# Where VectorE sums k, who makes a quarter of the local probabilities' copies, and how the tail of k is copied: attention and mixture of experts on one core

## The chip, the core and the metric

The kernel runs on one core of a Trainium2 chip. The core has five engines, each with its own in-order queue: TensorE (PE: matrix products and transposes, with its weight loads, PEld, beside them), VectorE (DVE), ScalarE (ACT), GpSimd (POOL) and SyncE (SP, which issues most transfers). [...] The metric is the time of one execution on the device in microseconds, the median of several runs.

## The reference

Two stages. Attention for 8 batch elements, 8 heads, 576 positions of 64 numbers: a local part, in which a position sees only its neighbours less than 4 away, and a coarse part over sums of 4 positions, whose output is repeated four times. Then a mixture of 8 experts: each of the 4,608 rows goes to the expert with the largest gate.

```python
q_d, k_d, v_d = (x.reshape(B, H, Sd, 4, D).mean(axis=3) for x in (q, k, v))
out_up = np.repeat(sm_attn(q_d, k_d, v_d), 4, axis=2)
mask = np.abs(pos[:, None] - pos[None, :]) < 4
scores = np.where(mask, scale * np.matmul(q, k.transpose(0, 1, 3, 2)), -1e9)
attn = softmax(scores)                    # max, exp, sum + 1e-09
x = rows(out_up + np.matmul(attn, v))
e_idx = argmax(x @ w_gate + modality_bias[modality_id])
out[e_idx == e] = gate * (np.maximum(x[e_idx == e] @ w1[e], 0) @ w2[e])
```

## The kernel before

**Steps.** Attention goes in 32 steps, n = 4b + hp, four for each batch element b. The work of one step is spread over almost four step times: while step n's q and k are transposed, step n − 1 has its scores, n − 2 its normalization and n − 3 its output. In the notes below the name in brackets is that of the method (and of the tile in the profile).

- PE transposes q and k into PSUM (tp, L275), four blocks each. ScalarE copies them to SBUF, q scaled (qT, L295) and k in two copies of 64x512, one for each half of the partitions (kT, L307). VectorE sums each four neighbouring columns of the same PSUM tile of k (kd, L321; in the call list kd0). The 64 columns that are left over at the end of each step are transposed for two steps together (tpt, L288); ScalarE copies k's part in four copies of 64x64 (L304 and L305), VectorE sums it (kd1, L317).
- The coarse scores (scd, L376) need kd and POOL's sums of q (qe L327, qd L331). VectorE takes their maximum (dm, L381), ScalarE the exponential with its sums (de, L389), POOL the division (nd, L407, which writes de), PE transposes (pdt, L428), ScalarE copies to SBUF (PdT, L436), and PE multiplies with v's sums (vp L263, copied by VectorE to vd at L268; avd L443).
- The local scores (mask and sc, L341 and L349) are 32 wide windows. VectorE takes maximum and difference (lm L356, le L362), ScalarE the exponential (L367), VectorE the sums and their reciprocal (z L393, zr L398 and L399), POOL the product with it (nl, L403, which writes le), VectorE transposes blocks of 32x32 (lt, L414). Then ScalarE makes four copies of 32 partitions each (Pw, L419, j from 0 to 3) into a tile that is zero elsewhere, and PE multiplies with v (avl, L458). VectorE adds coarse and local part (X, L469, a piece of it named late).
- In every fourth step the router runs for a finished batch element: logits (lg L505), copied by ScalarE (LT, L512) and transposed (lgt, L518); VectorE's chain of small operations (L524 to L563, from L to w and so on), PE's ranks (pr, L570 to L574), slots (sl and si, up to L586), and POOL's scatters of row numbers (tab, L615), four or five for a batch element; VectorE transposes rows (R, L600), SP stores them.

**Order.** The order of each engine's queue is not left to a scheduler. `PHASE` gives each method of a step a due time in units of steps; `call(n + p, ...)` collects all calls, and the list is sorted by time and issued in that order, so an engine's queue holds its instructions in the order of their due times. For VectorE the fractions of one step run: zr 0.29, R 0.30, kd0 0.30, lm1 0.34, le1 0.37, L and ch1 0.44 to 0.49, lt 0.508, dm 0.509, kd1 0.54, ch2 0.56, vc 0.66, X 0.66 and 0.69, lm0 0.73, le0 0.84, z 0.90. For POOL: nl 0.45, nd 0.60, qe and qd 0.62, between them scatters at 0.00, 0.20, 0.59 and 0.62 of certain steps.

**Buffers.** PSUM tiles of tag T (three buffers) serve the transposes: tp, tpt, vp, pdt, lgt. A buffer comes free when its last reader is done; for k's transposes that is ScalarE's copies and VectorE's sums. Reads of one PSUM tile by two engines are kept apart by the framework: kd begins when kT's second copy is done.

**After attention**, from about 260 us on, the expert units run: PE does three passes for each product (high and low parts of both factors).

Of the kernel before, what the change touches and what calls it, by code (L numbers as in the profile page):

```python
# [7 lines left out]
F32 = mybir.dt.float32  # L8
# [14 lines left out]
SUB, WIN, KEYS = 24, 32, 30  # L23
BLK = 4 * SUB
NB = 6
PAD = 3
KT = S - SUB + WIN
# [17 lines left out]
NPW = 3  # L45
# [8 lines left out]

PHASE = {
# [22 lines left out]
class Consts:  # L78
    def __init__(s, tc, pool, psum):
        nc = tc.nc  # L80

        s.ps = psum
        pool.tile([128, 48], F32, name="pad")
        s.dummy = pool.tile([128, 128], BF16, name="dummy")
        nc.vector.memset(s.dummy, 0.0)
        s.busy(nc, 12)
        s.ident = pool.tile([128, 128], F32, name="ident")
        make_identity(nc, s.ident)
        s.identb = pool.tile([128, 128], BF16, name="identb")
        make_identity(nc, s.identb)  # L90

        x = pool.tile([128, 1], F32, name="warm")
        nc.vector.memset(x, 0.0)
        nc.scalar.activation(x, x, AF.Exp)
        m = pool.tile([128, WIN], BF16, name="band")
        nc.gpsimd.memset(m, 0.0)
        for j in range(4):
            t = m[32 * j : 32 * j + 32]
            nc.gpsimd.affine_select(out=t, in_=t, pattern=[[1, WIN]], compare_op=ALU.is_ge, fill=NEG, base=0,
                                    channel_multiplier=-1)  # L100
            nc.gpsimd.affine_select(out=t, in_=t, pattern=[[-1, WIN]], compare_op=ALU.is_ge, fill=NEG, base=6,
                                    channel_multiplier=1)
        s.mask = pool.tile([128, NB, WIN], BF16, name="mask")
        nc.vector.tensor_copy(s.mask, m.unsqueeze(1).broadcast_to([128, NB, WIN]))
        nc.vector.memset(s.mask[0:32, 0:2, 0:PAD], NEG)
        s.band = m

        s.pool = pool.tile([128, 32], F32, name="pool")
# [84 lines left out]
class Attention:  # L193


    def __init__(s, tc, ctx, ectx, C, psum, q, k, v):
        s.tc, s.C, s.ps = tc, C, psum
        nc = s.nc = tc.nc
        s.q, s.k, s.v = q, k, v

        s.ld = ectx.enter_context(tc.tile_pool(name="ald", bufs=2, side="right", reuse_waits="tile"))
        s.wk = ctx.enter_context(tc.tile_pool(name="awk", bufs=2, reuse_waits="tile"))
        s.one = ctx.enter_context(tc.tile_pool(name="aone", bufs=1, reuse_waits="tile"))
        s.QK, s.t = {}, {}
        s.vw = [(s.ld, s.one)[j].tile([128, H * NB, D], F32, name=f"vw{j}", bufs=1) for j in range(2)]

        s.qT2 = s.ld.tile([128, 2, S], F32, name="qT", bufs=1)
        s.kB = s.ld.tile([128, 2, 2, KT], F32, name="kT", bufs=1)
        nc.vector.memset(s.kB, 0.0)
        s.mask = s.one.tile([128, NB, WIN], BF16, name="mask")  # L210
        nc.vector.tensor_copy(s.mask, C.band.unsqueeze(1).broadcast_to([128, NB, WIN]))
        nc.vector.memset(s.mask[96:128, NB - 2 :, SUB + PAD : WIN], NEG)
        s.Pw = [s.one.tile([128, 2 * NB, 4, SUB], F32, name=f"Pw{j}") for j in range(NPW)]

        s.De = [s.one.tile([128, 3, 32 * NB], F32, name=f"de{j}") for j in range(3)]
        for j in range(2):
            (nc.vector, nc.gpsimd)[j].memset(s.vw[j], 0.0)

        for j in range(3):
            nc.vector.memset(s.De[j], 0.0)  # L220
# [76 lines left out]
    def kT_(s, n, i):  # L297
        g = n % 2
        p = s.t["tp", "t"][:, 1] if i else s.t["tp", "k", n]
        for a in range(2):  # L300
            r = slice(64 * a, 64 * a + 64)
            if i:
                t = s.kB[r].rearrange("m g a t -> m g (a t)")[:, :, KT * a + PAD : KT * a + PAD + 512 + 64]
                s.nc.scalar.copy(t[:, 0, 512:], p[r, :64])  # L304
                s.nc.scalar.copy(t[:, 1, :64], p[r, 64:])  # L305
            else:
                s.nc.scalar.copy(s.kB[r, g, a, PAD + 64 * g : PAD + 64 * g + 512], p[r])  # L307

# [107 lines left out]
    def Pw_(s, n, j):  # L416

        r = slice(32 * j, 32 * j + 32)
        s.nc.scalar.copy(s.Pw[n % NPW][r, :, j, :SUB], s.t["lt", n][r, :, :SUB])  # L419

    def pdt(s, n, i):

# [850 lines left out]
```

## Time and profile before

| | us |
|---|---|
| median of 3 runs | 694.59 |
| lowest, highest | 693.19, 696.73 |
| the profiled execution | 696.98 |
| its span, first to last instruction | 695.3 |
| PE busy | 649.5 (93%) |
| DVE busy | 403.1 (58%) |
| ACT busy | 379.9 (55%) |
| POOL busy | 238.6 (34%) |

The shares are of the whole span and mix two stages. The attention stage takes the first 260 us, the expert units the rest. Times in the views are microseconds from the span's start. In lists of instructions a line is: start, duration, engine, line of the kernel, operation, out<-in, shape of out<-shape of in, count, and in brackets the idle time of that engine before it with what ended it. Matmuls are pipelined, so a busy PE isn't at its peak.

### The profile page before, as it was taken

The page shows a single profiled execution, that of the slowest core. Times are in us where ns is not written, and L with a number is a line of the kernel's source. Part 1 is how long each engine was busy: PE and PEld are TensorE (multiplying, and loading weights), DVE is VectorE, ACT ScalarE, POOL GpSimd, SP SyncE. Part 2 cuts the span into 40 slices and gives each one's busy share as a digit, 9 for nine tenths or more (in the row PEclk, how much of TensorE's full clock was granted, in tenths as well). Part 3 has the DMA queues.
Part 4 walks back from the last instruction along what each step waited for, and adds up shares of the span by engine and source line. Part 5 has one row for each costly group of instructions (what it writes and reads, how often), then busy time and mean ns, then how long its engine had stood idle before and what let it go on. Part 6 is the DMA issues. An engine that isn't in the chain of part 4 may idle for free. (4 is left out here: it accounts for less than half of the span.)

```text
span 695.3 us, 16717 instructions
## 1 busy us (share of the span) xinstructions
PE 649.5 (93%) x6123; PEld 518.3 (75%) x6123; DVE 403.1 (58%) x938; ACT 379.9 (55%) x884; POOL 238.6 (34%) x302
## 2 busy tenths in 40 slices
PE   7898999888988889998999999999999999999896
PEld 4576666666656667886888888888888888889794
DVE  6688898888879886746444234323452343416610
ACT  4798998887888754452444334433443243425710
POOL 6644563635476564360220300403204012210111
PEclk9899999999999999999999999999999999999999
DMA  9899889998887938397561544616524345155700
GB/s 186 171 179 195 161 182 194 157 206 146 159 172 166 200 81 219 99 309 221 153 210 45 169 152 121 192 51 185 179 81 122 131 137 181 53 136 171 221 29 31
DMA packets 176423, 106.99 MB, mean 154 GB/s; under 512 B 136300, under 2 KB 154770, under 8 KB 176338
## 3 DMA queue, kind: packets, MB, share of 16 engines
q1 hardware_dynamic: 169138, 86.71, 53.9%
q0 software_dynamic: 7200, 19.18, 8.6%
q8 instruction: 50, 0.82, 0.5%
q14 instruction: 35, 0.29, 0.2%
HBM read 86.61 MB, written 19.51 MB: 153 GB/s over the span
## 5 line engine op out<-in xcount | busy, mean ns | idle before, releaser
L833 DVE TENSOR_TENSOR wlo<-raw,whi 128x1024 fp32r<-128x1024 f32 x73 | 87.9, 1227 | 79.6 <-ACT whi L827 72.4
L977 POOL DMA_INDIRECT out_dram<-o,tg x34 | 37.1, 1091 | 250.2 <-ACT o L969 194.6
L923 DVE SCALAR_TENSOR_TENSOR hl<-l,hh 128x512 fp32r<-128x512 f32 x72 | 49.5, 688 | 105.4 <-ACT hh L922 101.7
L922 ACT ACTIVATE hh<-l 128x512 fp32r<-128x512 f32 x72 | 42.6, 596 | 109.8 <-PE l L918 108.2
L966 PE MATMUL l<-whi,hh 128*128 128x512 f32 x256 | 100.2, 395 | 1.9 <-ACT hh L947 1.9
L966 PE MATMUL l<-whi,hl 128*128 128x512 f32 x256 | 99.9, 391 | 0.0
L966 PE MATMUL l<-wlo,hh 128*128 128x512 f32 x256 | 99.8, 391 | 0.0
L918 PE MATMUL l<-xh,whi 128*128 128x512 f32 (+1 forms) x256 | 95.1, 375 | 2.1 <-DVE hl L923 2.1
L918 PE MATMUL l<-xl,whi 128*128 128x512 f32 (+1 forms) x256 | 94.7, 370 | 0.0
L918 PE MATMUL l<-xh,wlo 128*128 128x512 f32 (+1 forms) x256 | 94.6, 370 | 0.0
L827 ACT CAST whi<-raw 128x1024 fp32r<-128x1024 f32 x70 | 71.5, 1051 | 29.6 <-DMA raw<-in_moe_w_dram 16.7
L969 ACT ACTIVATE o<-l,tg 128x512 f32<-128x512 f32 x37 | 25.4, 687 | 97.6 <-PE l L966 69.6
L403 POOL TENSOR_TENSOR le<-le,zr 128x384 f32<-128x384 f32 x32 | 26.6, 831 | 91.3 <-DVE zr L399 84.9
L966 PEld LDWEIGHTS l<-whi,hh 128*128 128x128 f32 x256 | 48.2, 188 | 11.8 <-ACT hh L947 2.2
L918 PEld LDWEIGHTS l<-xh,whi 128*128 128x128 f32 x256 | 48.1, 189 | 11.5 <-DVE hl L923 2.7
L419 ACT COPY Pw<-lt 32x288 f32<-32x288 f32 x128 | 54.5, 426 | 3.4 <-DVE lt L414 1.2
L966 PEld LDWEIGHTS l<-wlo,hh 128*128 128x128 f32 x256 | 48.2, 188 | 10.1
L966 PEld LDWEIGHTS l<-whi,hl 128*128 128x128 f32 x256 | 48.3, 189 | 9.5
L918 PEld LDWEIGHTS l<-xh,wlo 128*128 128x128 f32 x256 | 48.2, 188 | 8.3
L918 PEld LDWEIGHTS l<-xl,whi 128*128 128x128 f32 x256 | 48.3, 189 | 8.0
L896 DVE TENSOR_TENSOR xl<-xt,xh 128x512 fp32r<-128x512 f32 x37 | 24.3, 681 | 38.0 <-ACT xh L894 37.9
L615 POOL DMA_INDIRECT tab<-ig,si x36 | 38.5, 1068 | 20.7 <-DVE si L586 14.5
(245 smaller groups left out, 1297.7 us busy)
## 6 DMA issues: line engine op xcount, KB each, us to landing
raw<-in_moe_w_dram SPq DMA_DIRECT2D x176, 128.0 KB
raw<-in_moe_w_dram SPq DMA_DIRECT2D x44, 512.0 KB
vw<-in_v_dram SPq DMA_DIRECT2D x53, 180.0 KB
qt<-in_q_dram SPq DMA_DIRECT2D x30, 288.0 KB
kt<-in_k_dram SPq DMA_DIRECT2D x30, 288.0 KB
xs<-R SPq DMA_DIRECT2D x64, 128.0 KB
vw<-in_v_dram SPq DMA_DIRECT2D x15, 90.0 KB
xs<-R SPq DMA_DIRECT2D x12, 64.0 KB
```

Source lines behind the costliest of these rows:

```text
L403: s.nc.gpsimd.tensor_tensor(e, e, z[:, : 2 * NB].unsqueeze(2).broadcast_to([128, 2 * NB, WIN]), op=ALU.mult)
L419: s.nc.scalar.copy(s.Pw[n % NPW][r, :, j, :SUB], s.t["lt", n][r, :, :SUB])
L615: i = nc.gpsimd.indirect_dma_start(out=s.tab[:, :], out_offset=bass.IndirectOffsetOnAxis(ap=C.si[:, t : t + 1], axis=0), in_=C.ig[:, t, :] ...
L827: (nc.gpsimd.tensor_copy if turn <= 4 else nc.scalar.copy)(hi, raw)
L833: (nc.gpsimd if turn == 4 else nc.vector).tensor_tensor(lo, raw, hi.bitcast(F32), op=ALU.subtract)
L896: nc.vector.tensor_tensor(xl[:, :, hs], p, xh[:, :, hs].bitcast(F32), op=ALU.subtract)
L918: nc.tensor.matmul(p[:, f % n, :], a[:, fs], x[:, k, :N], start=(k == 0 and i == 0), stop=(k == 3 and i == 2))
L922: nc.scalar.activation(hh[:, g, :N], p, AF.Relu)
L923: nc.vector.scalar_tensor_tensor(hl[:, g, :N], p, 0.0, hh[:, g, :N].bitcast(F32), op0=ALU.max, op1=ALU.subtract)
L966: nc.tensor.matmul(p, a[:, f, hs], x[:, f % 2, :], start=(f == 0 and i == 0), stop=(f == 7 and i == 2))
L969: nc.scalar.mul(o, p, T[:, h, 1:2].bitcast(F32))
L977: nc.gpsimd.indirect_dma_start(out=s.out[:, :], out_offset=bass.IndirectOffsetOnAxis(ap=T[:, h, 0:1], axis=0), in_=o, in_offset=None, boun ...
```

## The change

Three edits. The due time of kd0 goes from 0.3000 to 0.5095, so in VectorE's queue the sum of k stands behind lt (0.5083) and dm (0.5093) of the same step. The copy j = 0 of Pw is issued on GpSimd instead of ScalarE, and its due time goes from 2.7494 to 2.6300, behind qd on POOL (0.6242). The tail of k is copied with two instructions instead of four: the tile of k gets 80 columns more at its end, so that one access with a stride of 656 columns reaches both halves g of the tail.

```diff
-    "kT1": 0.5356, ..., "kd0": 0.3000, "kd1": 0.5400,
+    "kT1": 0.5356, ..., "kd0": 0.5095, "kd1": 0.5400,
...
-    "nd": 2.5956, "vc": 2.6555, "Pw0": 2.7494, "pdt0": 2.7884,
+    "nd": 2.5956, "vc": 2.6555, "Pw0": 2.6300, "pdt0": 2.7884,
...
-        s.kB = s.ld.tile([128, 2, 2, KT], F32, name="kT", bufs=1)
-        nc.vector.memset(s.kB, 0.0)
+        s.kF = s.ld.tile([128, 4 * KT + 80], F32, name="kT", bufs=1)
+        nc.vector.memset(s.kF, 0.0)
+        s.kB = s.kF[:, : 4 * KT].rearrange("m (g a t) -> m g a t", g=2, a=2)
...
-                t = s.kB[r].rearrange("m g a t -> m g (a t)")[:, :, KT * a + PAD : KT * a + PAD + 512 + 64]
-                s.nc.scalar.copy(t[:, 0, 512:], p[r, :64])
-                s.nc.scalar.copy(t[:, 1, :64], p[r, 64:])
+                t0, w = KT * a + PAD + 512, 2 * KT - 512
+                t = s.kF[r, t0 : t0 + 2 * w].rearrange("m (g t) -> m g t", g=2)
+                s.nc.scalar.copy(t[:, :, :64], p[r].rearrange("m (g t) -> m g t", g=2))
...
-        s.nc.scalar.copy(s.Pw[n % NPW][r, :, j, :SUB], s.t["lt", n][r, :, :SUB])
+        (s.nc.scalar.copy if j else s.nc.gpsimd.tensor_copy)(s.Pw[n % NPW][r, :, j, :SUB], s.t["lt", n][r, :, :SUB])
```

KT is 584, PAD is 3, and NPW is 3 (three tiles of Pw in turn).

4 rows, old and new, of the table PHASE are left out of this document.

## The prediction

> **What bounds the kernel now.** I read first the busy time by stage (columns: stretch in us, its length, then busy us with the number of instructions for PE, PEld, DVE, ACT, POOL, then granted clock, DMA share, GB/s).
>
> ```profile
> 32.00:240.00 208.00, 184.07 (x3508) 135.75 (x3506) 180.48 (x563) 179.11 (x560) 114.93 (x150) 0.98 0.92 176
> 240.00:262.00 22.00, 18.73 (x267) 14.15 (x264) 18.42 (x49) 13.37 (x40) 12.79 (x11) 0.92 0.46 114
> 262.00:695.30 433.30, 422.54 (x2028) 352.35 (x2027) 182.85 (x272) 169.89 (x233) 90.76 (x91) 0.99 0.48 144
> ```
>
> All that the change touches lies before 262 us. Behind it PE is busy for 422.5 of 433.3 us and nothing else comes near, so what the attention stage gains or loses should arrive at the end nearly whole. In the attention stage (32 to 240 us) PE, DVE and ACT are busy 184, 180 and 179 of 208 us: three in-order engines at 86 to 88%, none of them the sole bound. POOL has room: 115 of 208.
>
> So the question is who ends PE's idle time there, 208 − 184 = 24 us and 3.3 more up to 262. That was the second view, the waits from 32 to 262 us (engine and line that waited, for whom, us in total, times, longest).
>
> ```profile
> POOL le L403 <- DVE zr L399: 83.4, 22, 8.2
> DVE kd L321 <- ACT kT L307: 13.8, 13, 2.2
> ...
> PE pdt L428 <- POOL de L407: 5.8, 9, 1.9
> ...
> PE lgt L518 <- ACT LT L512: 5.2, 6, 0.9
> ...
> PE avl L458 <- ACT Pw L419: 3.8, 7, 0.8
> PE tp L275 <- ACT PdT L436: 3.4, 8, 1.4
> ...
> PE pr L570 <- DVE X L469: 1.7, 4, 0.4
> ...
> PE pr L570 <- DVE late L469: 1.4, 3, 0.5
> ```
>
> The 13.8 us in which VectorE waits with kd for ScalarE's copy of the same PSUM tile is what the change removes. It isn't PE's time, though. PE's own waits are five: 5.8 us for POOL's division of de, 5.2 for the router's LT (untouched by the change), 3.8 for Pw, 3.4 for PdT, and 1.7 + 1.4 = 3.1 in the router's pr, seven times, once for each of seven batch elements, for VectorE's X. The change can only pay or cost in these.
>
> **kd moves behind lt and dm.** The third view is the order of time around a step with n mod 4 = 3, in which the router's chain runs (start, us, engine, line, operation; in brackets the idle time before it).
>
> ```profile
> 112.84 0.69 DVE L321 TENSOR_REDUCE kd<-tp 128x128 f32<-128x512 f32 x1 [1.16 <-ACT kT L307]
> ...
> 113.26 0.44 PE L518 MATMUL lgt<-ident,LT 128*128 128x128 f32 x2 [0.86 <-ACT LT L512]
> 113.45 0.35 DVE L356 TENSOR_REDUCE lm<-sc 128x6 f32<-128x192 f32 x1
> ...
> 114.10 0.34 DVE L524 TENSOR_REDUCE L<-lgt 128x16 f32<-128x64 f32 x2
> ...
> 114.27 0.95 PE L376 MATMUL scd<-kd,qd 64*64 64x144 f32 x12
> ...
> 115.53 0.57 DVE L381 TENSOR_REDUCE dm<-scd 128x3 f32<-128x432 f32 x1
> 116.03 0.16 DVE L545 TENSOR_SCALAR w<-L 128x32 f32<-128x32 f32 x1
> ...
> 117.22 0.82 DVE L469 TENSOR_TENSOR X<-avl,Od 128x288 f32<-128x288 f32 x2
> ...
> 117.73 0.18 PE L570 MATMUL pr<-oh,tri 128*128 128x32 bf16 x1 [0.43 <-DVE X L469]
> ```
>
> Here kd costs VectorE 113.45 − 112.84 = 0.61 us from its start to the next start, behind 1.16 us of waiting. Take both away and what is late next is L, which cannot start before lgt ends at 113.26 + 0.44 = 113.70. From L to dm the order takes 115.53 − 114.10 = 1.43 us, so dm could start at about 113.75 + 1.43 = 115.18; but scd ends only at 114.27 + 0.95 = 115.22, so dm starts at about 115.27, 0.26 us sooner than now. Behind dm there now stands kd, 0.61 us, ahead of w, X and the rest. X therefore comes 0.61 − 0.26 = 0.35 us later, and PE already waits for X in pr. kd stood in a hole; the change puts it into the stretch that PE waits for. Seven batch elements times 0.35 us: **+2.5 us**. X and all that follows it on VectorE (down to zr, for which POOL waits) move by the same 0.35, so this isn't counted again at pdt.
>
> In a step with n mod 4 = 2 there is a hole too, and dm follows scd at once:
>
> ```profile
> 106.11 0.95 PE L376 MATMUL scd<-kd,qd 64*64 64x144 f32 x12
> ...
> 107.11 0.61 DVE L381 TENSOR_REDUCE dm<-scd 128x3 f32<-128x432 f32 x1
> ...
> 107.90 0.68 DVE L268 COPY vd<-vp 96x512 f32<-96x512 f32 x1
> ...
> 109.17 0.60 PE L275 MATMUL tp<-ident,qt 128*128 128x128 f32 x4
> ```
>
> dm starts 0.05 us behind the end of scd (107.06), so nothing can come sooner, and vd, which frees a PSUM buffer of the transposes, ends 0.61 us later, at 107.90 + 0.68 + 0.61 = 109.19, where the next transpose now starts at 109.17. With the 0.05 us that dm stood behind scd as a semaphore's delay, that costs 0 to 0.15 us in each of seven steps; I take 0.05: **+0.3 us**. The tile of k's transposes is held longer as well: kd would end at about 107.11 + 0.61 + 0.69 = 108.4, and pdt, the next user of such a buffer, stands right ahead of tp at 109.17 and takes about half a us, so I cost it at nothing; without that spare time it is the second rival's. In the other two steps of four kd starts without a wait, and moving it changes only what stands ahead of it: lt and dm come 0.61 us sooner, kd1 and the rest when they did. The wait for ScalarE's copy itself is gone everywhere: even in the router's step that copy ended by 112.84, where it released kd, 2.7 us ahead of dm.
>
> **ScalarE loses a quarter of Pw and half of the tail's copies.** Prices, from the groups by line (count, then busy us, mean ns of one):
>
> ```profile
> L419 ACT COPY Pw<-lt 32x288 f32<-32x288 f32 x128 | 54.5, 426 | 3.4 <-DVE lt L414 1.2 <-issue 0.6
> ...
> L307 ACT COPY kT<-tp 64x512 f32<-64x512 f32 x64 | 37.0, 578 | 1.0
> ...
> L327 POOL TENSOR_TENSOR qe<-qT 128x288 f32<-128x288 f32 x32 | 22.3, 698 | 10.1 <-ACT qT L293 5.7 <-ACT kT L304 4.3
> ...
> L305 ACT COPY kT<-tpt 64x64 f32<-64x64 f32 x32 | 6.8, 212 | 0.0
> ...
> L1028 POOL COPY X<-late 128x256 f32<-128x256 f32 x4 | 1.6, 395 | 0.0
> ```
>
> 32 copies of Pw leave: 32 × 0.426 = 13.6 us of ScalarE. The tail's copies go from 64 to 32; one of 64x128 lies between the rows of 64x64 and 64x512, 212 + 64 × (578 − 212)/448 = 264 ns, an estimate, so 64 × 0.212 − 32 × 0.264 = 5.1 us leave. Together 18.7 us, some 0.6 us in each step. On PE's path that can shorten two waits, avl for Pw (3.8 us) and tp for PdT (3.4 us). The first ends in a step like this (with POOL's rows beside PE's):
>
> ```profile
> 97.56 0.43 POOL L331 TENSOR_TENSOR qd<-qe 128x144 f32<-128x144 f32 x1
> ...
> 99.15 0.85 POOL L403 TENSOR_TENSOR le<-le,zr 128x384 f32<-128x384 f32 x1
> ...
> 100.16 1.00 POOL L615 DMA_INDIRECT tab<-ig,si  x1 [0.17 <-issue]
> ...
> 100.40 1.21 PE L458 MATMUL avl<-Pw,vw 128*64 128x96 f32 x24 [0.59 <-ACT Pw L419]
> ...
> 101.18 0.93 POOL L407 TENSOR_TENSOR de<-de,zr 128x432 f32<-128x432 f32 x1
> ...
> 102.16 0.39 PEld L428 LDWEIGHTS pdt<-ident,de 64*96 64x96 f32 x12 [0.25 <-POOL de L407]
> ```
>
> Here avl's 0.59 us would go, and PE would then stand 0.59 us longer before pdt, which waits for POOL's de at 101.18 + 0.93 = 102.11. Nothing is gained in such a step. In others pdt has some room, and at the end of the stage avl is the last to wait. I take half of the 3.8 us: **−1.9 us**; bounds 0 and −3.8. Of the 3.4 us for PdT I take a third, since tp comes later by vd as shown: **−1.2 us**; bounds 0 and −3.4.
>
> **POOL gains 32 copies.** No row shows this copy on POOL. The nearest is its 128x256 copy, 395 ns; the two-input qe of 288 elements, 698 ns, is an upper bound, and ScalarE's own 426 lies near the first. I take 0.42 us, as a copy of 288 is 12% more than one of 256. It waits for lt, and on POOL the scatters of the routing and the next step's nl are queued behind it. In the step above POOL runs without a hole from 97.56 to 102.11, the copy goes in behind qd, and pdt comes 0.42 us later. That run is longest where five scatters fall on it, with every second batch element, three times: 3 × 0.42 = **+1.3 us**; bounds 0 and 7 × 0.42 = 2.9. In the router's step the copy waits for lt instead:
>
> ```profile
> 113.59 0.42 POOL L331 TENSOR_TENSOR qd<-qe 128x144 f32<-128x144 f32 x1
> 113.96 0.39 POOL L1028 COPY X<-late 128x256 f32<-128x256 f32 x1
> 120.76 0.83 POOL L403 TENSOR_TENSOR le<-le,zr 128x384 f32<-128x384 f32 x1 [6.41 <-DVE zr L399]
> ```
>
> lt stands right ahead of dm, which starts at 115.5 now, so POOL stands for up to 1.5 us behind qd's end at 114.0; behind it are only that copy of late, wanted four steps on, and nl, which waits for VectorE until 120.7. This costs nothing.
>
> **The sum.** +2.5 + 0.3 − 1.9 − 1.2 + 1.3 = +1.0 us. The profiled execution took 696.98 us (span 695.3), 2.4 more than the median of the runs, 694.59; it would take 698.0, and the median becomes **695.6 us**.
>
> **Rivals.** First, faster: ScalarE and the wait at kd are the true bound, and VectorE, rid of 13.8 us of standing, is ahead whenever PE wants it. For it: three engines at 87%, and avl, tp and kd all wait for ScalarE. Against it: where kd stood longest, the next thing on VectorE waits for PE anyway. It gives 3.8 + 3.4 = 7.2 us back with no cost at all: 687.4.
>
> Second, slower: kd stands on the path of every batch element and ScalarE's relief is swallowed whole at pdt. The place is pdt behind POOL's de; the price for a batch element is 0.35 (X), 0.15 (vd) and 0.42 (POOL's copy), seven times, 2.5 + 1.0 + 2.9 = 6.4: 701.0. It decides once VectorE reaches zr later than now and POOL has no hole before nl. For it: the 5.8 us of pdt are PE's longest wait. Against it: POOL waits 22 times for zr, 83.4 us, so most of its copies find room.
>
> Third, POOL's copy could land beside a VectorE subtraction of two SBUF tiles:
>
> ```profile
> 232.47 1.56 DVE L833 TENSOR_TENSOR wlo<-raw,whi 128x1024 fp32r<-128x1024 f32 x1
> ...
> 232.91 1.64 POOL L327 TENSOR_TENSOR qe<-qT 128x288 f32<-128x288 f32 x1
> ```
>
> This qe took 1.64 us while wlo ran, where the mean of all 32 is 0.70. Such subtractions fall only on the last steps; if three copies of Pw met one, 3 × 0.94 = 2.8 us more than forecast: 698.4. [...]
>
> That the change doesn't do what it says can hardly be: the order is written out by hand, and each copy is one instruction.
>
> **How the numbers follow.** Forecast 0.42; first rival 0.32, as three engines so evenly loaded often gain more from relief than single steps show; second 0.22; third 0.04. 0.5%, about 3.5 us, is what a measurement of this kernel can tell from no change. The forecast's own cases (its bounds are unlikely to fall together) stay within it, the first rival is faster, the other two are slower: 0.32, 0.42, 0.26. The range reaches to both ends, 687.4 and 701.0, rounded to 687.5 and 701.
>
> **What would show it.** Right: kd without a wait for kT; dm in router steps within 0.1 us of the end of scd; pr's wait for X up from 3.1 to about 5 us; avl's for Pw below 2; Pw0 on POOL near 0.42 us; ScalarE's busy time down by 19 us. Wrong, towards faster: pr's wait no longer and pdt's below 5.8 us. Wrong, towards slower: pdt's wait at 8 us or more, or a new wait of tp for vd.

## The result and the profile after

The changed kernel takes 698.16 us (median of 17 runs, 695.74 to 704.85), the kernel before 695.74 in its 17 runs (691.58 to 698.22). The medians lie 2.4 us apart, the means 4.1. The ratio on record is 1.0062, with a 95% interval of 1.0039 to 1.0085: about 0.6%, or 4 us, slower, just beyond the 0.5% that the prediction named as what can be told from no change. The forecast was 695.6 and no change as the likeliest case; the range of 687.5 to 701 holds the result.

The busy time by stage of the kernel after, to be read against the first view of the prediction (its profiled execution took 698.16 us with a span of 696.5):

```profile
32.00:240.00 208.00, 184.03 (x3523) 137.01 (x3521) 179.90 (x561) 170.18 (x503) 125.68 (x177) 0.98 0.91 174
240.00:262.00 22.00, 17.06 (x247) 12.54 (x244) 18.55 (x49) 11.54 (x35) 13.94 (x15) 1.00 0.49 132
262.00:696.50 434.50, 420.98 (x2025) 350.21 (x2023) 181.92 (x270) 169.35 (x233) 91.60 (x91) 1.00 0.47 143
```

In the attention stage PE is as busy as before, ScalarE 9 us less, POOL 11 us more. The surprise is the last row: behind 262 us, where no line of the diff does anything, PE now stands idle for 434.50 − 420.98 = 13.5 us, before for 433.30 − 422.54 = 10.8.

The waits from 32 to 262 us after:

```profile
POOL le L404 <- DVE zr L400: 63.8, 20, 6.7
...
PE lgt L519 <- ACT LT L513: 5.6, 7, 0.9
...
POOL Pw L420 <- DVE lt L415: 5.0, 6, 1.1
PE pdt L429 <- POOL de L408: 4.9, 10, 1.1
...
PE pr L571 <- DVE X L470: 3.6, 4, 1.2
...
PE tp L276 <- ACT PdT L437: 3.1, 2, 2.8
...
PE pr L571 <- DVE late L470: 2.9, 3, 1.0
...
PE avl L459 <- ACT Pw L420: 2.7, 4, 0.7
...
PE avl L459 <- issue: 1.2, 2, 0.9
...
PE avl L459 <- POOL le L404: 0.7, 1, 0.7
```

kd's 13.8 us of waiting for kT are gone, and PE's wait in pr has gone from 3.1 to 3.6 + 2.9 = 6.5 us. pdt's wait for POOL went down by 0.9 us, and tp's for PdT is nearly one stall of 2.8 us. avl's wait for Pw seems to be down by a third (3.8 to 2.7), but the view puts other waits of avl down to POOL's le and to no releaser (issue), and in those too ScalarE's last copy of Pw had ended just 0.1 us before. All of PE's idle time ahead of avl was 5.0 us before and is 4.7 after. The groups by line show the price of the moved and merged copies:

```profile
L420 ACT COPY Pw<-lt 32x288 f32<-32x288 f32 x96 | 41.1, 429 | 1.5
...
L420 POOL COPY Pw<-lt 32x288 f32<-32x288 f32 x32 | 14.9, 465 | 5.1 <-DVE lt L415 5.0
...
L306 ACT COPY kT<-tpt 64x128 f32<-64x128 f32 x32 | 8.2, 257 | 0.4
```

And the router's step, in the order of time, as in the third view of the prediction:

```profile
114.37 0.95 PE L377 MATMUL scd<-kd,qd 64*64 64x144 f32 x12
...
115.38 0.60 DVE L382 TENSOR_REDUCE dm<-scd 128x3 f32<-128x432 f32 x1
...
115.89 0.68 DVE L322 TENSOR_REDUCE kd<-tp 128x128 f32<-128x512 f32 x1
...
116.49 0.17 DVE L546 TENSOR_SCALAR w<-L 128x32 f32<-128x32 f32 x1
...
117.70 0.82 DVE L470 TENSOR_TENSOR X<-avl,Od 128x288 f32<-128x288 f32 x2
118.20 0.18 PE L571 MATMUL pr<-oh,tri 128*128 128x32 bf16 x1 [0.80 <-DVE X L470]
```

dm starts 0.06 us behind the end of scd (115.32), kd fills 0.60 us between dm and w, and pr starts 118.20 − 115.32 = 2.88 us behind scd. Before it was 117.73 − 115.22 = 2.51: 0.37 later, where 0.35 was worked out.

### The profile page after: what moved, and what is told of

It is laid out like the page before. It is cut to its first block, busy times and chain, and to the rows that moved or that the text cites. A ratio compares the mean times of both kernels' runs of the same rounds, so it can differ in the third digit from the quotient of the medians.

```text
span 696.5 us, 16672 instructions
## 1 busy us (share of the span) xinstructions
PE 646.8 (93%) x6123; PEld 516.4 (74%) x6123; DVE 403.4 (58%) x938; ACT 368.7 (53%) x820; POOL 252.5 (36%) x334
## 5 line engine op out<-in xcount | busy, mean ns | idle before, releaser
L459 PE MATMUL avl<-Pw,vw 128*64 128x96 f32 x768 | 39.2, 250 | 5.4 <-ACT Pw L420 3.5
```

The costliest lines, as they stand in the source:

```text
L459: s.nc.tensor.matmul(p[64 * a : 64 * a + 64, c], vw[:, NB * (4 * (hp // 2) + hp % 2 + 2 * a) + k, :], Pw[:, 2 * k + a], start=True, stop=T ...
```

## Experiments

Twelve runs of ten kernels, in three sets of four; each set on a chip of its own, with the kernel before run beside it (medians 692.77, 698.77 and 698.91), so only ratios are compared between sets. pw_only's profiled execution took 707.66 us, 6 above its median, so only its ratio is used.

The table puts them together. "13 steps" is the time from the first transpose of step n = 4 to that of n = 17 in the trace; in that stretch executions of equal work agree to 0.1 us (kd_router's has one stall of 1.2 us more, in n = 11). It holds the router's steps n = 7, 11 and 15. "pr" is PE's wait there for X and late (32 to 262 us). "Stretch" is a piece of the expert stage, some 284 to 330 us. It starts with the 96th matmul of l1, the last of the first expert unit's first product, and ends with the 97th of l2 (the expectations call it the 96th), the first of the second unit's second product. The 96 matmuls of the first unit's l2 take 22.2 to 22.3 us of it in every trace; what differs lies behind them, in 72 matmuls of the second unit's l1.

| kernel | ratio, 95% interval | 13 steps | pr | stretch |
|---|---|---|---|---|
| before | | 92.38 | 3.1 | 42.4 |
| after | 1.0062 [1.0039, 1.0085] | 93.80 | 6.5 | 45.6 |
| kd_only | 1.0072 [1.0045, 1.0100] | 94.33 | 6.9 | 45.0 |
| no_kd | 0.9992 [0.9960, 1.0023] | 92.01 | 3.6 | 43.1 |
| kd040 | 1.0017 [0.9988, 1.0046] | 91.53 | 3.7 | 46.9 |
| tail_only | 0.9946 [0.9914, 0.9977] | 91.82 | 3.0 | 42.2 |
| kd_router | 1.0045 [1.0014, 1.0076] | 94.65 | 6.1 | 45.2 |
| pw_only | 1.0029 [0.9996, 1.0063] | | | |
| kd040_tail | 1.0058 [1.0024, 1.0092] | 91.35 | 3.1 | 45.7 |
| tail_again | 0.9995 [0.9968, 1.0022] | 91.86 | 3.4 | 40.5 |
| kd_5 | 1.0031 [1.0004, 1.0058] | 92.33 | 3.2 | 44.4 |
| kd_r6 | 1.0013 [0.9982, 1.0044] | 93.61 | 5.2 | 41.4 |
| after_old | 1.0038 [1.0004, 1.0073] | 93.80 | 5.7 | 42.4 |
| tail_third | 0.9961 [0.9933, 0.9989] | 91.85 | 3.6 | 43.6 |

The theory at first was that of the prediction: kd stands ahead of X in the router's steps. The rival was that POOL's copies cost the time.

**The parts one by one.** kd_only moves kd alone, in the kernel before.

```diff
-"kd0": 0.3000, "kd1": 0.5400,
+"kd0": 0.5095, "kd1": 0.5400,
```

> Only kd0 moves (0.30 to 0.5095); Pw and the tail as before. If kd on the router step's path is the cost: PE's wait in pr for VectorE's X goes from 3.1 to between 5.5 and 6.5 us, and the time rises by 2.5 to 3.5 us (ratio 1.0035 to 1.005). If the cost comes from POOL's copies or from the expert stage: no change (within 1 us), pr's wait notwithstanding.

Its ratio is 1.0072, as much as the whole change costs; in size (5.0 us), and with 6.9 us of waiting in pr, it is above the upper ends expected. no_kd is the change without this edit (kd0 back at 0.3000):

> The change without the move of kd0: Pw's quarter on POOL and the two-copy tail. If kd is the cost: 0 to 2 us faster than before (ratio 0.997 to 1.000), pr's wait back at about 3 us, kd waiting for kT again by some 13 us. If POOL's copies or the expert stage are the cost: still 3 to 4 us slower than before (ratio 1.005).

0.9992: nothing clear of noise is left of the loss. So kd's place carries it, and the rival falls as the cause of the whole; what POOL's copies cost by themselves is taken up with pw_only. kd040 has the whole change with kd0 at 0.4000, in the hole ahead of dm:

```diff
-"kd0": 0.5095, "kd1": 0.5400,
+"kd0": 0.4000, "kd1": 0.5400,
```

> The whole change, but kd0 at 0.40: behind lm1 and le1, ahead of L, lt and dm. If the hole ahead of L is what kd needs: kd ends before the second lgt in the router step, dm follows scd by 0.05 us, X comes 0.26 us sooner than before, pr's wait falls to about 1.5 us (3.1 less 7 times 0.26) and the time is 1 to 3 us under before (ratio 0.996 to 0.9985). If kd's place doesn't matter: as no_kd.

What kd had added to pr's wait is gone, but it is 3.7 us, not the expected 1.5, and the 13 steps are 0.48 us shorter than no_kd's. Yet the whole is not faster than no_kd (1.0017), nor than before, where 0.996 to 0.9985 was expected. So kd's move must cost something outside the router's steps too. tail_only has the two tail copies and the 80 columns alone, the third edit of the diff above:

> Only the tail of k in two copies and the 80 columns more. If ScalarE is off PE's path: within 0.7 us of before, ScalarE's busy time down by about 5 us. If the 80 columns disturb what is allocated later for the experts: 2 to 4 us slower, with PE's waits growing between 310 and 330 us.

0.9946, or 3.7 us less, where 0.7 us at most was expected. ScalarE's busy time fell by 2.4 us, its durations in sum by 4.9, where about 5 was expected.

**Where kd's move costs.** Two candidates were left: X in the router's steps, and the longer stretch in the expert stage, which all three kernels with kd moved had shown in their traces.

```diff
-    call(n + p, values if f == "X" else ...
+    call(n + p + (0.2095 if nm == "kd0" and n % 4 == 3 else 0), values if f == "X" else ...
```

> Only one number of the whole change: kd stands at 0.5095 in the steps whose X the router waits for (n mod 4 = 3), and at 0.30 in all others; Pw and the tail as before. The theory that the loss is kd ahead of X: PE's wait of pr for X and late comes to 6 to 7 us (3.1 before, 6.9 with kd moved everywhere), router steps are 0.37 to 0.50 longer each, 7 of them make 2.6 to 3.5 us, so a ratio of 1.0035 to 1.006, and the stretch from the 96th l1 matmul to the 96th l2 matmul is as before (42 to 43 us). The rival, that most of the 5.0 us of kd moved alone lies elsewhere (0.8 in the step from n = 5 to 6, 2.6 in the expert stage): pr's wait is as long, and yet the ratio is at most 1.002.

1.0045 with a pr wait of 6.1 us. But the stretch is 45.2 us, although kd is moved only within attention: the first theory's ratio with the rival's stretch, so this run alone doesn't tell them apart. pw_only has only the first Pw copy on POOL (with its due time of 2.6300):

```diff
-    s.nc.scalar.copy(s.Pw[n % NPW][r, :, j, :SUB], s.t["lt", n][r, :, :SUB])
+    (s.nc.scalar.copy if j else s.nc.gpsimd.tensor_copy)(s.Pw[n % NPW][r, :, j, :SUB], s.t["lt", n][r, :, :SUB])
```

> Only the first Pw copy on POOL; kd at 0.30 and four tail copies. The difference between no_kd and tail_only, +3.2 us, would be POOL's copy: then this is 1.003 to 1.005, with pr's and zr's chains 0.4 later in n = 11 and 27 and 0.39 more in the step from n = 13 to 14. The rival, that without the tail's saving ACT is the later engine and the copy that it loses pays for POOL's: 0.999 to 1.0015, avl's wait for Pw 2.8 as in no_kd, against 3.8 before.

1.0029, with an interval that holds no change: not settled. kd040_tail joins the tail's copies with kd0 at 0.4000:

> Two tail copies and kd at 0.40, all Pw copies on ACT. The theory that X then waits for PE's avl and the 0.26 us that dm gains are not passed on: within 0.003 of tail_only, so 0.992 to 0.997, pr's wait for X and late 3.0 to 3.7. The rival, that moving kd lengthens the expert stage by about 3 us wherever it is put (45 to 47 us from the 96th l1 to the 96th l2 in the three kernels with kd moved): 0.998 to 1.001 and 45 us or more there.

1.0058, against tail_again's 0.9995 in the same set. The 13 steps are the shortest of all, 91.35; the stretch is 45.7. The ratio lies above both expectations. The rival was right that moving kd lengthens the expert stage wherever kd is put, but its price of about 3 us doesn't give all of this loss. tail_again:

> The two tail copies alone, once more. If its gain is the kernel's: 0.992 to 0.997 again, and a stretch from the 96th l1 to the 96th l2 matmul within 1 us of 42.2. The rival, that the gain was of one set of runs: 0.998 to 1.001; and if that stretch is 44 us or more here, its length is scatter between executions and not the work of kd.

0.9995: the gain of tail_only is not confirmed, and a third measurement was needed. Its stretch of 40.5 is the shortest of all, so the stretch scatters by up to 3 us with the same order (40.5 to 43.6), and only the gap between the two groups counts.

**What lengthens the expert stage.** The code answers it. Attention's calls are issued within `manual_schedule()`, in the order of their due times. What follows isn't: the framework orders the last batch's routing and the expert units, with `high_priority()` on some. The lists of instructions show two such orders. All six kernels with the long stretch have one, the same for each instruction of PE and, in the expert stage, of VectorE; the others have that of before, but for a few places on PE and ScalarE. Between the two, PE's list differs in 20 lines by the names in the traces (the expectation of kd_5 counts 64). Moving kd in the single step n = 5 is enough to get the other order. In the whole change, leaving kd in place in the steps n mod 4 = 1 is enough to keep the old one (after_old); it isn't in general, since kd_router leaves it in place there too and has the new order. Presumably the plan starts from the planned ends of attention; that was not tried by itself.

What the new order does is read on VectorE, before and then in kd_only (the last batch's slots, from sl to si):

```profile
278.49 0.19 DVE L582 TENSOR_TENSOR sl<-pr,ecap 128x40 f32<-128x40 f32 x1
...
281.58 0.19 DVE L585 TENSOR_REDUCE sf<-sl 128x5 f32<-128x40 f32 x1
281.85 1.23 DVE L833 TENSOR_TENSOR wlo<-raw,whi 128x1024 fp32r<-128x1024 f32 x1
...
283.22 0.16 DVE L586 CAST si<-sf 128x5 int32<-128x5 f32 x1
```

```profile
278.84 0.19 DVE L582 TENSOR_TENSOR sl<-pr,ecap 128x40 f32<-128x40 f32 x1
...
281.97 1.23 DVE L833 TENSOR_TENSOR wlo<-raw,whi 128x1024 fp32r<-128x1024 f32 x1
...
283.33 0.19 DVE L585 TENSOR_REDUCE sf<-sl 128x5 f32<-128x40 f32 x1
284.19 1.23 DVE L833 TENSOR_TENSOR whl<-raw,whl 128x1024 fp32r<-128x1024 f32 x1 [0.67 <-ACT whl L827]
...
286.15 0.16 DVE L586 CAST si<-sf 128x5 int32<-128x5 f32 x1
```

From sl to si it takes 7.31 us instead of 4.73: one weight split more (1.23 us) stands between them, and VectorE waits twice for ScalarE's part of a split (0.64 and 0.67 us). POOL's scatters into the table, the gathers that read it and the scatters of results follow on POOL (kernel before, then kd_only):

```profile
283.65 1.03 POOL L615 DMA_INDIRECT tab<-ig,si  x1 [14.50 <-DVE si L586]
...
302.57 1.31 POOL L977 DMA_INDIRECT out_dram<-o,tg  x1 [0.30 <-issue]
```

```profile
286.60 2.04 POOL L615 DMA_INDIRECT tab<-ig,si  x1 [17.17 <-DVE mn L748]
...
306.70 2.00 POOL L977 DMA_INDIRECT out_dram<-o,tg  x1 [0.30 <-ACT whi L827]
```

Each result scatter frees one of three buffers "o", and one of these is wanted by VectorE's table for the last units (L652), with weight splits and hl queued behind it. In nine of the 13 traces the profile names the scatter's transfer as what ended VectorE's wait there; in the others, kd_only among them, it names nothing. Here are that row and the later ones in kd_only, and PE's wait for it:

```profile
314.65 0.42 DVE L652 TENSOR_TENSOR o<-ltri,mn 128x256 f32<-128x256 f32 x1 [6.86 <-issue]
...
316.21 1.22 DVE L833 TENSOR_TENSOR wlo<-raw,whi 128x1024 fp32r<-128x1024 f32 x1
...
317.49 1.22 DVE L833 TENSOR_TENSOR wlo<-raw,whi 128x1024 fp32r<-128x1024 f32 x1
...
318.69 0.69 DVE L923 SCALAR_TENSOR_TENSOR hl<-l,hh 128x512 fp32r<-128x512 f32 x1
```

```profile
319.43 0.72 PE L918 MATMUL l<-xh,whi 128*128 128x512 f32 x1 [3.27 <-DVE rcnt L768]
```

The view puts this wait down to rcnt, which runs beside hl's end; hl, which reads PE's results in PSUM, ends at 319.38, 0.05 us before PE goes on. In kernels that keep the old order, si starts 1.4 to 2.8 us ahead of the first l2 matmul (seven traces); with the new order 0.9 to 1.9 us behind it (six traces). The rest of the chain follows in all 13: from the start of the stretch, the first gather starts at 11.5 to 14.2 us with the old order and 15.6 to 17.0 with the new, the second result scatter at 16.8 to 19.9 and 21.2 to 22.8, and L652 at 25.6 to 28.7 and 28.3 to 31.0.

PE's idle time in the stretch is 1.7 us on average with the old order (0.4 to 2.8) and 4.0 with the new (3.3 to 4.8). One stall of 3.3 to 3.4 us like kd_only's is in four of the six. In after it is only 0.98, and two waits for hl (1.32 and 1.87) make up most; kd040 is alike, with 1.72 for ScalarE's whi and 2.18 for hl. In four of the six, against one of the seven, the stretch also holds 3.4 us at half clock (a granted clock of about 0.5). To test it by time, kd_5 moves kd in one step alone and so takes over the new order with attention left nearly as it was:

```diff
-    call(n + p, values if f == "X" else ...
+    call(n + p + (0.2095 if nm == "kd0" and n == 5 else 0), values if f == "X" else ...
```

> kd at 0.5095 in one step alone, n = 5; in the 31 others at 0.30, Pw and the tail as before. No X that the router waits for is touched, but the order of the expert units, which no due time sets, comes out as in all kernels with kd moved (64 lines of difference in PE's order, none against kd_only). The theory that this order costs time of its own: 45 to 47 us from the 96th l1 to the 96th l2 matmul (45.0 to 46.9 in the five kernels with kd moved, 40.5 to 43.6 in the five without), PE's wait in pr 3.1 as before, and 2 to 3.5 us in all, a ratio of 1.003 to 1.005. The rival, that the loss is kd ahead of X and the longer stretch comes of other things (loads, the clock): a stretch of 40.5 to 43.6 and 0.9985 to 1.0015.

1.0031, 92.33 us for the 13 steps (before 92.38), pr 3.2, and a stretch of 44.4: a little under the expected 45 but outside all traces of the old order. By the ratio that is 2.2 us for the order alone (0.3 to 4.1); the medians are only 1.0 us apart. kd_r6 does the converse, kd late in router's steps with the old order:

```diff
-    call(n + p, values if f == "X" else ...
+    call(n + p + (0.2095 if nm == "kd0" and n % 4 == 3 and n < 27 else 0), values if f == "X" else ...
```

> kd at 0.5095 in six of the seven steps with a router (n = 3 to 23), in all others at 0.30; with these the expert units keep their order of before (PE's order is the same line by line). The theory of the prediction, kd ahead of X: 6 times 0.37 to 0.50, so 2.2 to 3.0 us, a ratio of 1.003 to 1.0045, pr's wait for X and late 5.5 to 6.5, 40.5 to 43.6 us from the 96th l1 to the 96th l2. The rival, that only the new order of the expert units costs: pr's wait as long, but the ratio at most 1.0015.

One thing in that expectation was miscounted: the step n = 3 has no router's chain, so five chains are touched, not six. Five times 0.37 to 0.47 is 2.1 us. The trace has the 13 steps 1.23 us longer, 0.41 for each of three, pr at 5.2, and the stretch at 41.4. The time says 0.9 us, with an interval (−1.3 to 3.1) that holds 2.1 and also nothing. kd_5 and kd_r6 together make 1.0044, kd_router, which has both causes, 1.0045; the widths of the intervals make this agreement weak. after_old is the whole change with the old order:

```diff
-    call(n + p, values if f == "X" else ...
+    call(n + p - (0.2095 if nm == "kd0" and n % 4 == 1 else 0), values if f == "X" else ...
```

> The whole change, but kd left at 0.30 in the steps with n mod 4 = 1; all seven router steps have it at 0.5095. With this the expert units are ordered as with kd at 0.30 everywhere (no difference to no_kd in PE's and ACT's order). If the order of the expert units costs some 3 us of the whole change's 1.0062: 1.001 to 1.003, and 42 to 43.5 us from the 96th l1 to the 96th l2, with pr's wait still 6 to 7. If kd ahead of X is all of it: 1.005 to 1.007.

1.0038 with a stretch of 42.4: between the two expectations, and pr's wait of 5.7 us is a little under the 6 expected. It is 1.7 us less than the whole change took, but in another set and with intervals that overlap. A stall ahead of the stretch, 2.2 us of PE waiting for a gather at 270 us, is in this one trace. tail_third:

> The two tail copies alone a third time, because 0.9946 and 0.9995 don't settle whether they gain. If the gain is there: 0.9945 to 0.998. If it was one chip's: 0.9985 to 1.001. In both the order of the expert units is that of before, so 40.5 to 43.6 us from the 96th l1 to the 96th l2.

0.9961. Three ratios, 0.9946, 0.9995 and 0.9961, have a mean of 0.9967, 2.3 us less. Two of three intervals lie below 1, and the 13 steps are 0.52 to 0.56 us shorter in all three traces. Two tail copies alone are so, by the ratios, the best of these kernels, ahead of both given ones. kd040_tail has the shortest 13 steps; with the old order of the expert units it should avoid the long stretch too, but which of kd's due times would keep that order there was not tried, and no such kernel was run.

## Why the prediction was right and where it failed

**The range held, in part by luck.** Of the sum's terms the router's +2.5 us was right; a cost of about 3 us in the expert stage was missing, and the 3.1 us of relief from ScalarE did not show in the waits that they were taken from. The range reached far enough because of the second rival, whose mechanism did not come. Put together from the runs: 7 × 0.4 = 2.8 us for X, 2.2 to 3.2 for the new order, 0.5 once in step 5 (below) and no_kd's −0.6 make 4.9 to 5.9, where the ratio says 4.3 (2.7 to 5.9).

**The router's steps: right.** +0.35 us for each X, seven times, was forecast. In kd_router, pr starts 0.37 to 0.47 us later behind scd in six of seven steps (the sixth 0.59), the 13 steps of kd_r6 give 0.41 each. pr's wait came to 6.5 us instead of "about 5"; by the prediction's own sum, 3.1 + 2.5, it should have been 5.6.

**"All that the change touches lies before 262 us": this step failed.** It was taken from the diff. The order behind 262 us is planned, and the change altered the plan. The stretch that it lengthens took 42.2 us on the average of seven traces with the old order (40.5 to 43.6) and 45.5 in six with the new one (44.4 to 46.9): +3.2 us, 2.2 in the time of kd_5. This is the term that the sum lacked, put at nothing. "The order is written out by hand" was true of attention alone.

**kd elsewhere.** In the step from n = 5 to 6 kd_only and after take 7.22 us, the kernel before 6.44. Two things make up the 0.8 us. With kd moved in n = 5 alone (kd_5) the step takes 0.27 more, and the next one 0.33 less. With kd moved in n = 4 but not in n = 5 (after_old) it takes 0.50 more: there PE's matmul mp (L180), which sets up the router's biases once, waits 0.86 us for VectorE's mf (L178), in kd_only 0.78, in the kernel before 0.14 and for ScalarE. kd stands ahead of mf as it stands ahead of X, so the prediction's "kd1 and the rest when they did" failed here. No wait of tp for vd came up in after, for which 0.3 us was counted.

**POOL's copy: price right, total open.** 0.42 us was the estimate, though 12% more than 395 ns is 0.44; the median of the 32 copies is 415 ns. One of them, from 233.58 to 235.51 us, took 1.93 us (hence the mean of 465), and beside it a weight split ran on VectorE from 234.0 to 235.2. That is the third rival's case, once instead of three times and 1.5 us long instead of 0.94; no_kd has one of 1.79 us. No other copy in after ran beside a split, and none took over 0.44 us. The copy on POOL costs 0.39 us in the step from n = 13 to 14, in each of after, no_kd, kd040 and after_old. But the 13 steps with Pw on POOL as well as the tail (no_kd) are 0.37 us shorter than before and only 0.15 to 0.19 longer than with the tail alone. By time, no_kd against tail_only is +3.2 us, pw_only by itself +2.0 (−0.3 to 4.4). Whether that is more than the forecast +1.3 minus its relief isn't settled.

**ScalarE's relief: right in size, wrong in place.** Its instructions' durations sum to 18.6 us less, forecast 18.7 (the merged copy 257 ns, forecast 264). The page's busy time fell only from 379.9 to 368.7, as ScalarE's instructions often overlap, mostly by about 0.1 us (451 times before, 388 after), and busy time counts an overlap once. The two waits that were to shrink by 3.1 us shrank by 1.4 in after by the view's names (avl 3.8 to 2.7, tp 3.4 to 3.1), and avl's by 0.3 if all its waits are counted. tail_only has avl at 4.5 and tp at 3.3, and is faster all the same: its steps n = 7, 9, 11 and 15 are 0.1 to 0.3 us shorter each. So the relief was argued from the wrong waits, and the part of the gain outside these steps was not traced.

**The rivals.** The forecast of no change, within 0.5%, was missed by little: the ratio is 0.6%, its interval 0.4 to 0.85%. The slower rival had the sign, and its price (+6.4) was above the 4 us measured. But its mechanism, ScalarE's relief swallowed at pdt, is not what happened: pdt's wait fell to 4.9 us. The faster rival fell with kd_only: kd's 13.8 us of waiting were no bound.

**The hole at 0.40.** There kd does no harm to X: pr comes 2.28 to 2.46 us behind scd in kd040 and kd040_tail (five and six of seven steps), 0.05 to 0.23 sooner than before. That was the gain to be had at this place, about 1 us in all, less than the new order of the expert units costs.

## What to carry to other kernels

When an engine's wait is filled by work from behind it, ask who waits for what now stands later: kd's 1.2 us of waiting ahead of dm cost PE nothing, the same 0.6 us of work between dm and X cost it 0.4 in every batch element. Where part of a program is ordered by hand and the rest by a planner, compare the lists of instructions of the whole program before arguing that a change ends where its diff ends; one due time in step 5 reordered the expert units. And test an edit to such a program as a bundle of two, the edit and the new plan: a variant that has the plan without the edit (kd_5) prices it, as far as the noise allows.

## What the runs showed of the hardware

In these traces a stall of PE often cost more than its length. In kd_only the wait of 3.27 us is followed at once by 3.41 us at a granted clock of 0.51, half clock in what follows (columns as in the first view; the granted clock is the third number from the end):

```profile
316.20:319.50 3.30, 0.07 (x1) 0.07 (x1) 3.30 (x9) 1.54 (x2) 0.17 (x1) 1.00 1.04 277
319.50:322.91 3.41, 3.41 (x8) 2.70 (x9) 1.73 (x3) 0.77 (x1) 0.00 (x0) 0.51 1.01 371
```

In 13 traces (all but pw_only's), PE stood idle 20 times for 2.1 us or more between 32 us and the end; 18 times a stretch at half clock began 1.7 to 5.3 us behind the start of the gap, of 3.41 us or two or three times that. Of the 15 gaps of 1.5 to 2.0 us it followed three in this way. Not every such stretch had a long gap ahead of it: of 32 stretches at half clock in those traces, 11 had only shorter gaps in the 6 us before, each up to 1.4 us and 1.3 to 3.0 in all. In kd_only's 3.41 us PE has 8 matmuls, in the 3.09 us behind them, at a granted clock of 0.99, 15. Such a stretch costs PE 1.7 us more when PE is the bound, an estimate from its length and clock, 3.41 × (1 − 0.51).

The largest scatter between executions has one place. POOL's first weight split stands in its hand-written queue near 226 us, ahead of a le and a de, and in tail_again its load came late; these are the waits of POOL and of PE there:

```profile
POOL whi L828 <- DMA raw<-in_moe_w_dram: 6.8, 1, 6.8
```

```profile
PE pdt L429 <- POOL de L408: 7.3, 1, 7.3
```

The granted clock was 0.50 from 228.0 to 238.2 us, from within those 7.3 us (225.0 to 232.3) on, and PE was busy for 5.90 us of that stretch. In the other traces PE's longest wait for de lies between 1.0 and 7.9 us. That is as large as everything that this change moves. It may be one reason why the intervals above are as wide as they are; that was not tested.
